# Attention matmuls pinned among the layers' units, and a query side laid out by unit

## The chip, the cores and the metric

The kernel runs on one core of one Trainium2 chip. The metric is the device time of one execution in microseconds (us). Engines: PE is TensorE's matmul, PEld its weight load, DVE is VectorE, ACT is ScalarE, POOL is GpSimd, SP is SyncE, which issues the DMAs.

## The reference

Linear attention over 4 batches of 8 heads, 576 positions, head size 64, followed by two feed-forward layers on the 2304 tokens:

```python
def phi(x):
    proj = x @ w_phi                                   # 64 -> 128
    proj = proj - max(abs(proj), axis=-1)
    return concat([exp(proj), exp(-proj)])             # 256 features
q_p, k_p = phi(q), phi(k)
kv  = k_p^T @ v ;  z = sum_s k_p                       # per batch and head
attn = (q_p @ kv) / (q_p @ z + 1e-6)
x  = attn as (tokens, 512)
x  = leaky_relu(x @ w_in, 0.01) @ w_out                # 512 -> 2048 -> 512
out = (silu(x @ w_gate) * (x @ w_val)) @ w_out2        # 512 -> 1536 -> 512
```

The weights of the two layers arrive as 64-bit floats, everything else as 32-bit floats.

## The kernel before, in words

**Units.** The layers are cut into 272 units, in an order written out by hand (lines 620 to 658): per batch 16 units of the first product (`u_l1`), 12 pairs of gate and value units (`u_gate`, `u_val`), and after every fourth hidden block four units of the output product (`u_out`). Every unit is 24 matmuls of 128x288 in two halves of 12 (`products`, line 543), each half into one of the four PSUM buffers of the tag `pm`; the second half's first matmul opens its second buffer. Operands are kept as a rounded part and a remainder, and three of the four products of parts are made. Batch 0 owns units 0 to 63, batch 1 units 64 to 131, batch 2 132 to 199, batch 3 200 to 267; the last four finish batch 3.

**Weights.** In batch 0 every weight block comes as 64-bit numbers and is turned to 32 bits and split by ACT and DVE (`w_to_f32`, lines 504 to 522: two ACT and three DVE instructions of 128x512; `w_split`, lines 524 to 532: one of each), about one block a unit, up to four units ahead of its use. From batch 1 on the split blocks are read back from DRAM, so this work is gone.

**Attention.** Batch 0 is computed before unit 0. Batches 1 to 3 are computed beside the units of the batch before. The key side (`k_steps`, line 249) has 24 steps: `k_front` makes one block of features (PE, then DVE for the maximum, ACT for the exponentials), `k_back` two steps later sums it into the key-value product, `k_z` and `k_tr` finish a head pair. Batch 1 keeps its operands whole (`whole`, line 103), so each of its feature matmuls shows as two records; batches 2 and 3 split them. The query side of batches 1 to 3 (`q_steps_t`, line 439) goes over 8 groups (4 head pairs by 2 halves of the positions): `q_p` projects (line 334 and 335, two banks) and turns the result on DVE; `q_m_t` forms the maximum: one small matmul (line 344), four DVE instructions (lines 346 to 354) that end in the tile `mrow`; `q_exp` subtracts it by a matmul (line 365) and takes two exponentials on ACT (lines 373 and 374); `q_num` multiplies with the key-value product (line 391); `q_fin` divides.

**PSUM.** The attention of batches 1 to 3 uses four buffers of the tag `pa` (`bk`, line 93). `q_p` holds two of them from its matmul until the exponentials of `q_exp` have read them; each `q_num` holds one until `q_fin` has read it.

**Where the steps stand.** `spread` (line 685) gives each step a unit after which it is written: for batch 1 the key steps behind units 0 to 23 and the query steps behind units 24 to 60; for batches 2 and 3 behind the first 32 units of the batch before and the 33 that follow. `q_steps_t` makes 20 steps, two per group (`q_p` and `q_m_t` of one group, `q_exp` of the group before, `q_num` of the one before that), so a step is 1.85 units in batch 1 and 1.65 in the others.

**What sets the order.** A planner orders each engine's instructions. It takes, of those that its own timeline holds ready, the one with the lowest priority number, which is the place in the program; attention steps are written with the number lowered by 50 (line 718). An issue-order token keeps all instructions that carry it in program order on their engine. Before the change only the first matmul of each half unit carries the token "units":

```python
m = pe.matmul(ps, w, x[:, c], start=(i == 0), stop=(i == n - 1))
if i == 0:
    tc.stamp_issue_order_token(m.ins, "units")
```

So the units stay in order among themselves, and an attention matmul may go ahead of its place or behind it. On the chip every engine then runs its list in order.

Of the kernel before, what the change touches and what calls it, by code (L numbers as in the profile page):

```python
# [19 lines left out]
F = 128  # L20
# [19 lines left out]
def linear_attention_two_mlps(ctx: ExitStack, tc, qT, kT, vt, w_phi, w1, w2, wg, wv, w3, cst, out):  # L40
# [35 lines left out]
    def constants():  # L76
# [13 lines left out]
        dve.tensor_copy(sel, signs)  # L90
        dve.tensor_scalar(out=ones, in0=zero, scalar1=1.0, scalar2=None, op0=ALU.add)

    def bk(b=1):

        if b == 0:
            return T([P, 512], F32, "pm", 4, psm)
        return T([P, 512], F32, "pa", 4, psa)
# [51 lines left out]

    def k_front(b, j, s):  # L150
        ps = bk(b)
        o = slice(OFF[s], OFF[s] + P)
        pv = ps[:, 0 : 2 * F]
        if whole(b):
            ops = [(raw["k", b, j], wbd)]
        else:
            ops = [(kh[b, j], wbd_h), (kl[b, j], wbd_h), (kh[b, j], wbd_l)]
        for i, (a, w) in enumerate(ops):
            pe.matmul(  # L159
                pv, a[:, o], w.rearrange("p h f -> p (h f)"), start=(i == 0), stop=(i == len(ops) - 1)  # L160
            )
        pv = pv.rearrange("p (h f) -> p h f", h=2)
        mk = T([P, 2], F32, "mk", 2)
        dve.tensor_reduce(out=mk, in_=pv, axis=AX.X, op=ALU.max, apply_absolute_value=True)
        f = ff[b, j, s] = T([P, 2, 2, F], F32, "ff", 3)
        if b in (1, 2):
            mn = T([P, 2], F32, "mn", 2)
            dve.tensor_scalar(out=mn, in0=mk, scalar1=-1.0, scalar2=None, op0=ALU.mult)
            for h in range(2):
                act.activation(f[:, h, 0], pv[:, h], AF.Exp, bias=mn[:, h : h + 1])  # L170
                act.activation(f[:, h, 1], pv[:, h], AF.Exp, bias=mk[:, h : h + 1], scale=-1.0)
        else:
            d = f[:, :, 1]
            sub(d, pv, mk.rearrange("p (h o) -> p h o", o=1).to_broadcast([P, 2, F]))
            act.activation(f[:, :, 0], d, AF.Exp)
            act.activation(f[:, :, 1], d, AF.Exp, scale=-1.0)
        if whole(b):
            return
        hh = fh[b, j, s] = T([P, 2, 2, F], F32R, "fh", 3)
        ll = fl[b, j, s] = T([P, 2, 2, F], F32R, "fl", 3)  # L180
        cp(hh, f)
        sub(ll, f, hh.bitcast(F32))
        if s == 1:
            z = zacc[b, j] = T([P, 2, 2, F], F32, "zacc", 1)
            dve.tensor_tensor(out=z, in0=ff[b, j, 0], in1=f, op=ALU.add)
        elif s > 1:
            z = zacc[b, j]
            n = VAL[s]
            dve.tensor_tensor(out=z[:n], in0=z[:n], in1=f[:n], op=ALU.add)

    def k_back(b, j, s):
        if s == 0:
            kvp[b, j] = bk()
        ps = kvp[b, j]
        n = VAL[s]
        v = vaug.pop((b, j, s)) if whole(b) else vhl[b, j][:, s]
        for h in range(2):
            parts = (ff,) if whole(b) else (fh, fl)
            for i, part in enumerate(parts):
                pe.matmul(  # L200
                    ps[:, 256 * h : 256 * h + 256],
                    v[:n, h].rearrange("p a d -> p (a d)"),
                    part[b, j, s][:n, h].rearrange("p a f -> p (a f)"),
                    start=(s == 0 and h == 0 and i == 0),
                    stop=(s == NST - 1 and i == len(parts) - 1),
                    skip_group_check=True,
                )

    def z_split(b, j):
        if whole(b):  # L210
# [8 lines left out]
    def k_z(b, j):  # L219
        ps = kvp.pop((b, j))  # L220
        kz = kvz[b, j] = T([P, 512], F32, "kvz", 1)
        if whole(b):
            cp(kz, ps)
            return
        zh, zl = zhl.pop((b, j))
        tb = T([D, 512], F32, "ff", 3)
        cp(tb, ps[D:P])
        dve.tensor_tensor(out=kz[0:D], in0=ps[0:D], in1=tb, op=ALU.add)
        zp = bk()
        pe.matmul(zp, ones, zh, start=True, stop=False)  # L230
        pe.matmul(zp, ones, zl, start=False, stop=True)
        cp(kz[D:P], zp[D:P])

    def k_tr(b, j):
        kz = kvz.pop((b, j))
        ps = bk()
        for i in range(4):
            pe.transpose(ps[:, F * i : F * i + F], kz[:, F * i : F * i + F], ident)  # L238
        if whole(b):
            kvh[b, j] = T([P, 2, 2, P], F32, "kvh", 4)  # L240
            cp(kvh[b, j].rearrange("p h a f -> p (h a f)"), ps)
            return
        h = kvh[b, j] = T([P, 2, 2, P], F32R, "kvh", 4)
        l = kvl[b, j] = T([P, 2, 2, P], F32R, "kvl", 4)
        pv = ps.rearrange("p (h a f) -> p h a f", h=2, a=2)
        cp(h, pv)
        sub(l, pv, h.bitcast(F32))
# [78 lines left out]
    def q_p(b, j, t):  # L326

        c = slice(HT * t, HT * t + HT)
        tp = T([P, 2, NB, 32], F32, "pk", 5)
        for h in range(2):  # L330
            bank = pt[b, j, h, t] = bk(b)
            ps = bank[:, 0:HT]
            a = qs[b, j][h][:, c]
            pe.matmul(ps, wst_h, a, start=True, stop=False)  # L334
            pe.matmul(ps, wst_l, a, start=False, stop=True)  # L335
            dve.transpose(out=tp[:, h].rearrange("p a b -> p (a b)"), in_=ps)
        m = mq[b, j, t] = T([P, 2, NB], F32, "mqt", 2)
        dve.tensor_reduce(out=m, in_=tp, axis=AX.X, op=ALU.max, apply_absolute_value=True)

    def q_m_t(b, j, t):  # L340

        m = mq.pop((b, j, t)).rearrange("p h k -> p (h k)")
        turned = pt[b, j, 1, t][0 : 2 * NB, HT : HT + P]
        pe.matmul(turned, m, ident, start=False, stop=True, skip_group_check=True)  # L344
        top = T([2 * NB, 32], F32, "top", 2)
        dve.tensor_reduce(out=top, in_=turned.rearrange("r (g i) -> r i g", g=4), axis=AX.X, op=ALU.max)
        x = mm[2 + t]
        hi = x[0 : 2 * NB]
        dve.tensor_copy(hi, top)
        sub(x[32 : 32 + 2 * NB], top, hi.bitcast(F32))  # L350
        if t == 0:
            mrow[b, j] = T([P, 2 * NB, 32], F32R, "mrow", 1)
        r = mrow[b, j][:, NB * t : NB * t + NB]
        dve.tensor_tensor(
            out=r,
            in0=x.bitcast(F32).rearrange("p (o i) -> p o i", o=1).to_broadcast([P, NB, 32]),
            in1=mask_t.rearrange("p (k o) -> p k o", o=1).to_broadcast([P, NB, 32]),
            op=ALU.mult,
        )

    def q_exp(b, j, h, t):
        if lean(b):
            ps = pt.pop((b, j, h, t))[:, 0:HT]
            r = mrow[b, j][:, NB * t : NB * t + NB].rearrange("p k i -> p (k i)")
            pe.matmul(ps, sel[:, 2 + h], r, start=False, stop=True, skip_group_check=True)  # L365
        else:
            ps = bk()[:, 0:HT]
            c = slice(HT * t, HT * t + HT)
# [14 lines left out]
    def q_num(b, j, h, t):  # L383
# [4 lines left out]
        if not whole(b):  # L388
            ops += [(kvl[b, j][:, h, s], hh[:, s]) for s in range(2)]
        for i, (w, x) in enumerate(ops):  # L390
            pe.matmul(ps, w, x, start=(i == 0), stop=(i == len(ops) - 1))  # L391
        if h == 0:
            dn[b, j, t] = T([P, HT], F32, "dn", 2)
        act.activation(dn[b, j, t][D * h : D * h + D], ps[D:P], AF.Copy, bias=1e-6)  # L394
# [20 lines left out]
        sub(xl[b, j][:, c], x, xh[b, j][:, c].bitcast(F32))  # L415

    def q_steps(b):
        if lean(b):
            return q_steps_t(b)
        seq = []  # L420
        for j in range(NP):
            seq.append([lambda j=j: q_front(b, j, 0), lambda j=j: q_front(b, j, 1)])
# [13 lines left out]
            seq.append(prev)  # L436
        return seq

    def q_steps_t(b):


        groups = [(j, t) for j in range(NP) for t in range(2)]
        n = len(groups)
        steps = []
        for i in range(n + 2):
            one, two = [], []
            if i >= 2:
                j, t = groups[i - 2]
                one.append(lambda j=j, t=t: q_num(b, j, 0, t))
                two.append(lambda j=j, t=t: (q_num(b, j, 1, t), q_fin(b, j, t)))  # L450
            if 1 <= i <= n:
                j, t = groups[i - 1]
                one.append(lambda j=j, t=t: q_exp(b, j, 0, t))
                two.append(lambda j=j, t=t: q_exp(b, j, 1, t))
            if i < n:
                j, t = groups[i]
                if t == 0:
                    one.append(lambda j=j: q_split(b, j))
                one.append(lambda j=j, t=t: q_p(b, j, t))
                two.append(lambda j=j, t=t: q_m_t(b, j, t))  # L460
                if t == 1 and j + 1 < NP:
                    two.append(lambda j=j: load_q(b, j + 1))
                if t == 1 and j + 1 == NP and b + 1 < B:
                    two.append(lambda: load_k(b + 1, 0))
            steps += [one, two]
        return steps


    wtile, w64, wf = {}, {}, {}
# [220 lines left out]
    for b in range(B - 1):  # L690
        first, mid, end = bounds[b]
        if b == 0:
            mid -= 4
        spread(k_steps(b + 1), first, mid)
        spread(q_steps(b + 1), mid, end - 3)

    load_k(0, 0)
    steps = k_steps(0) + q_steps(0)
# [95 lines left out]
```

## Time and profile before

| | |
|---|---|
| median of 3 runs | 1112.93 us (1109.64 to 1115.9) |
| profiled execution | 1116.18 us, span 1114.3 us |
| PE, PEld busy | 1084.8 us (97%), 1047.4 us (94%) |
| DVE, ACT busy | 708.7 us (64%), 564.4 us (51%) |
| DMA | 203.60 MB, mean 183 GB/s |
| mean granted TensorE clock | 0.994 |

The shares are means over stages that differ: attention of batch 0 alone up to about 65 us; units 0 to 23 with the key side of batch 1 to 188 us; units 24 to 63 with its query side to 365 us; then batches 1 and 2 of the layers with the attention of batches 2 and 3; and from about 881 us layers alone. Busy time of PE includes the overlap of matmuls that follow each other, so a PE that is busy all the time may still have waited a little. A granted clock of 1.00 is 2.4 GHz, 0.50 is 1.2 GHz.

### The profile page before, as it was taken

The numbers are of one execution on the slowest core, as the hardware profiler recorded it, in microseconds if no ns is written. First come the engines' busy times: TensorE is split into PE (matmuls) and PEld (weight loads), VectorE is DVE, ScalarE is ACT, GpSimd is POOL, SyncE is SP. The second block draws the span as 40 slices with busy tenths as digits, with TensorE's granted clock in tenths as the row PEclk, the third lists the DMA queues.
The fourth block names the chain that finished last, engine by engine and source line by source line (L and its number), as shares of the span: only waits on it lengthen the run. The fifth ranks groups of instructions, "written<-read, shape, count | busy, mean of one in ns | idle before, by whom it ended". The sixth has DMA issues, their size and how long they took to land.

```text
span 1114.3 us, 19823 instructions
## 1 busy us (share of the span) xinstructions
PE 1084.8 (97%) x7728; PEld 1047.4 (94%) x7728; DVE 708.7 (64%) x1505; ACT 564.4 (51%) x1259; POOL 6.6 (1%) x28
## 2 busy tenths in 40 slices
PE   7899999999899999999999999999999999999998
PEld 6778999888898999999999999999999999999998
DVE  7887797998989656566675766637676412233233
ACT  7768886766657566544553466525543222222211
POOL 1000000000000000000000000000000000000000
PEclk9999999999999999999999999999999999999999
DMA  9626787667767843455342555434243454455541
GB/s 337 213 71 223 254 292 256 208 241 255 248 207 249 288 157 128 153 181 181 136 147 92 184 193 175 152 133 164 94 176 121 168 184 152 164 198 169 178 144 43
DMA packets 70476, 203.60 MB, mean 183 GB/s; under 512 B 17264, under 2 KB 17520, under 8 KB 70384
## 3 DMA queue, kind: packets, MB, share of 16 engines
q1 hardware_dynamic: 70384, 202.35, 52.6%
q8 instruction: 61, 1.00, 0.4%
q14 instruction: 31, 0.25, 0.1%
HBM read 159.86 MB, written 42.47 MB: 182 GB/s over the span
## 4 chain that ended last, share of the span: by engine, by line
PE 85%; DMA 5%; DVE 4%; ACT 4%; issue 1%; SPq 0%; ACTq 0%; DVEq 0%
PE pm L550 72%; PE pa L391 4%; PE pa L200 3%; DMA wi<-in_w_dram 2%; PE pa L159 2%; PE pm L299 1%; DVE wr L521 1%; PE pa L334 1%; PE pa L344 1%; PE pa L238 1%; PE pa L365 1%; DMA wi<-in_wv_dram 1%; DVE wr L516 1%; PE pa L335 1%; PE pa L370 0%
## 5 line engine op out<-in xcount | busy, mean ns | idle before, releaser
L550 PE MATMUL pm<-xh,wi 128*128 128x288 f32 x2560 | 539.3, 299 | 3.5 <-DVE es L581 1.1
L550 PEld LDWEIGHTS pm<-xh,wi 128*128 128x128 f32 x2560 | 420.3, 190 | 9.1 <-ACT xh L60 2.6
L550 PE MATMUL pm<-gp,wo 128*128 128x288 f32 x2688 | 389.5, 296 | 1.7 <-ACT wo L529 1.5
L550 PE MATMUL pm<-xl,wi 128*128 128x288 f32 x1280 | 379.8, 298 | 0.2 <-DVE xl L57 0.2
L550 PEld LDWEIGHTS pm<-gp,wo 128*128 128x128 f32 x2688 | 367.4, 188 | 5.1 <-ACT wo L529 1.8
L550 PEld LDWEIGHTS pm<-xl,wi 128*128 128x128 f32 x1280 | 242.5, 190 | 1.8 <-DVE xl L57 0.6
L57 DVE TENSOR_TENSOR gp<-es,gp 128x576 fp32r<-128x576 f32 x112 | 84.4, 753 | 98.4 <-ACT gp L60 98.1
L60 ACT ACTIVATE gp<-es 128x576 fp32r<-128x576 f32 x112 | 77.4, 691 | 92.5 <-DVE es L588 91.1
L607 DVE TENSOR_TENSOR acc<-pm,acc 128x288 f32<-128x288 f32 x160 | 70.6, 453 | 81.9 <-PE pm L550 81.3
L573 ACT ACTIVATE es<-pm 128x288 f32<-128x288 f32 x128 | 53.0, 417 | 104.2 <-PE pm L550 103.5
L588 DVE SCALAR_TENSOR_TENSOR es<-pm,es 128x288 f32<-128x288 f32 x96 | 43.3, 452 | 52.8 <-PE pm L550 52.1
L581 DVE SCALAR_TENSOR_TENSOR es<-es,pm 128x288 f32<-128x288 f32 x96 | 43.2, 450 | 34.1 <-ACT es L580 32.1
L57 DVE TENSOR_TENSOR fl<-ff,fh 128x512 fp32r<-128x512 f32 (+1 forms) x72 | 51.4, 716 | 18.5 <-ACT fh L60 17.5
L580 ACT ACTIVATE es<-pm 128x288 f32<-128x288 f32 x96 | 39.0, 409 | 41.8 <-PE pm L550 40.9
L514 ACT ACTIVATE wi<-wi 128x512 int32<-128x512 uint32 x62 | 43.0, 693 | 31.9 <-DMA wi<-in_w_dram 18.8
L60 ACT ACTIVATE fh<-ff 128x512 fp32r<-128x512 f32 (+1 forms) x72 | 47.5, 663 | 0.9
L394 ACT ACTIVATE dn<-pa 64x288 f32<-64x288 f32 x64 | 26.0, 406 | 42.3 <-PE pa L391 41.3
L513 ACT ACTIVATE wr<-wi 128x512 f32<-128x512 f32 x62 | 41.4, 689 | 11.3 <-DMA wi<-in_w_dram 7.2
L200 PE MATMUL pa<-ff,pk 128*128 128x256 f32 (+1 forms) x160 | 43.0, 384 | 4.0 <-issue 3.0
L521 DVE TENSOR_TENSOR wr<-wr,wi 128x512 uint16<-128x512 uint16 x62 | 46.2, 752 | 0.6
L60 ACT ACTIVATE acc<-pm 128x288 f32<-128x288 f32 x64 | 26.0, 422 | 33.4 <-PE pm L550 33.2
L516 DVE SCALAR_TENSOR_TENSOR wr<-wi,wr 128x512 int32<-128x512 int32 x62 | 42.3, 686 | 0.9
(107 smaller groups left out, 1183.6 us busy)
## 6 DMA issues: line engine op xcount, KB each, us to landing
wi<-kept SPq DMA_DIRECT2D x120, 512.0 KB, 3.5
wo<-kept SPq DMA_DIRECT2D x82, 512.0 KB, 5.4
wi<-in_w_dram SPq DMA_DIRECT2D x46, 512.0 KB, 5.0
kept<-wi SPq DMA_DIRECT2D x40, 512.0 KB, 4.2
kept<-wo SPq DMA_DIRECT2D x28, 512.0 KB, 4.9
wi<-in_wv_dram SPq DMA_DIRECT2D x12, 512.0 KB, 4.3
raw<-in_kT_dram SPq DMA_DIRECT2D x16, 288.0 KB, 3.2
raw<-in_qT_dram SPq DMA_DIRECT2D x16, 288.0 KB, 2.8
```

The costliest lines, as they stand in the source:

```text
L57: dve.tensor_tensor(out=o, in0=a, in1=b, op=ALU.subtract)
L60: act.activation(o, a, AF.Copy)
L200: pe.matmul(ps[:, 256 * h : 256 * h + 256], v[:n, h].rearrange("p a d -> p (a d)"), part[b, j, s][:n, h].rearrange("p a f -> p (a f)"), st ...
L391: pe.matmul(ps, w, x, start=(i == 0), stop=(i == len(ops) - 1))
L514: act.activation(low, low.bitcast(U32), AF.Copy, scale=2.0**-29)
L516: dve.scalar_tensor_tensor(out=ti, in0=high, scalar=-0x80000000, in1=ti, op0=ALU.bitwise_and, op1=ALU.bitwise_or)
L521: dve.tensor_tensor(out=t16, in0=t16, in1=e16, op=ALU.add)
L550: m = pe.matmul(ps, w, x[:, c], start=(i == 0), stop=(i == n - 1))
L573: act.activation(g[:, c], ps, AF.Prelu, alpha=0.01)
L581: dve.scalar_tensor_tensor(out=t[:, c], in0=t[:, c], scalar=1.0, in1=ps, op0=ALU.add, op1=ALU.mult)
L588: dve.scalar_tensor_tensor(out=g[:, c], in0=ps, scalar=0.5, in1=g[:, c], op0=ALU.mult, op1=ALU.mult)
L607: dve.tensor_tensor(out=acc[o][:, t], in0=ps, in1=acc[o][:, t], op=ALU.add)
```

## The change

`pinned` gives the token "units" to every attention matmul of batches 1 to 3: of the key side (`k_front`, `k_back`, `k_z`, `k_tr`) and of the query side (`q_p`, `q_m_t`, `q_exp`, `q_num`). Each then stands, in program order, behind the second half's first matmul of the unit after which it is written and ahead of the next unit's first matmul. The ACT, DVE and DMA instructions carry no new token.

The query side is no longer written as 20 steps. `q_places` gives each operation a place of its own, in periods of (hi - lo) / 8.5 units: 4.35 units in batch 1, 3.88 in batches 2 and 3. In periods from the group's start: `q_p` 0, `q_m_t` 0.27, both `q_exp` 0.75, `q_num` 1.27 and 1.47, `q_fin` 1.48. In batch 1 this puts `q_m_t` one unit behind `q_p`, `q_exp` two units behind `q_m_t` (three once), the first `q_num` two units behind `q_exp` (three once), and the next group's `q_p` one unit (two once) behind `q_exp`. Key steps keep their places.

```diff
+    def pinned(b, m):
+        if b:
+            tc.stamp_issue_order_token(m.ins, "units")
...
-            pe.matmul(
+            m = pe.matmul(
                 pv, a[:, o], w.rearrange("p h f -> p (h f)"), start=(i == 0), stop=(i == len(ops) - 1)
             )
+            pinned(b, m)
...
-            pe.matmul(ps, wst_h, a, start=True, stop=False)
-            pe.matmul(ps, wst_l, a, start=False, stop=True)
+            pinned(b, pe.matmul(ps, wst_h, a, start=True, stop=False))
+            pinned(b, pe.matmul(ps, wst_l, a, start=False, stop=True))
...
-    def q_steps_t(b):
+    def q_places(b, lo, hi):
         groups = [(j, t) for j in range(NP) for t in range(2)]
...
+        period = (hi - lo) / (len(groups) + 0.5)
+        out = []
+        for g, (j, t) in enumerate(groups):
+            if t == 0:
+                out.append((g, lambda j=j: q_split(b, j)))
+            out.append((g, lambda j=j, t=t: q_p(b, j, t)))
+            out.append((g + 0.27, lambda j=j, t=t: q_m_t(b, j, t)))
+            if t == 1 and j + 1 < NP:
+                out.append((g + 0.4, lambda j=j: load_q(b, j + 1)))
+            if t == 1 and j + 1 == NP and b + 1 < B:
+                out.append((g + 0.4, lambda: load_k(b + 1, 0)))
+            for h in range(2):
+                out.append((g + 0.75, lambda j=j, h=h, t=t: q_exp(b, j, h, t)))
+                out.append((g + 1.27 + 0.2 * h, lambda j=j, h=h, t=t: q_num(b, j, h, t)))
+            out.append((g + 1.48, lambda j=j, t=t: q_fin(b, j, t)))
+        out.sort(key=lambda p: p[0])
+        return [(int(lo + at * period), fn) for at, fn in out]
...
         spread(k_steps(b + 1), first, mid)
-        spread(q_steps(b + 1), mid, end - 3)
+        for at, fn in q_places(b + 1, mid, end - 3):
+            atts.setdefault(at, []).append([fn])
```

The matmuls of `k_back`, `k_z`, `k_tr`, `q_m_t`, `q_exp` and `q_num` are wrapped in the same way as those shown. No instruction is added or taken away on any engine.

## Rows read from the trace of the kernel before

**Rows 1.** Stages: stretch; busy us (instructions) of PE, PEld, DVE, ACT, POOL; clock; DMA.
```profile
65.00:125.00 60.00, 56.79 (x324) 48.83 (x324) 47.28 (x110) 47.28 (x129) 1.66 (x6) 1.00 0.54 180
125.00:188.00 63.00, 63.00 (x449) 61.62 (x448) 53.04 (x102) 51.06 (x114) 0.20 (x1) 1.00 0.83 294
...
202.00:365.00 163.00, 150.80 (x1009) 141.87 (x1008) 147.50 (x319) 106.22 (x217) 0.00 (x0) 0.96 0.69 237
365.00:484.00 119.00, 119.00 (x909) 118.65 (x908) 67.92 (x136) 67.56 (x171) 0.00 (x0) 1.00 0.54 189
484.00:622.00 138.00, 138.00 (x1029) 135.03 (x1028) 95.43 (x210) 62.56 (x135) 0.00 (x0) 1.00 0.42 137
...
900.00:1100.00 200.00, 200.00 (x1510) 199.97 (x1509) 58.94 (x111) 49.52 (x100) 0.00 (x0) 1.00 0.46 159
```

**Rows 2.** PE's waits, 202 to 365 us: total us, times, longest us.
```profile
PE pa L334 <- ACT ff L374: 4.4, 3, 3.2
PE pa L365 <- DVE mrow L354: 2.5, 1, 2.5
PE pm L550 <- ACT wo L529: 1.5, 1, 1.5
PE pa L391 <- DVE xf L409: 1.3, 1, 1.3
PE pm L550 <- DVE es L581: 1.1, 1, 1.1
```

**Rows 3.** Stage table again, three short stretches; the clock stands behind POOL.
```profile
243.40:246.70 3.30, 3.16 (x13) 3.16 (x14) 1.81 (x4) 3.27 (x9) 0.00 (x0) 0.50 0.72 288
304.90:311.60 6.70, 5.66 (x23) 5.67 (x24) 4.66 (x10) 6.32 (x13) 0.00 (x0) 0.50 0.52 191
352.70:356.00 3.30, 3.30 (x16) 3.30 (x15) 2.87 (x9) 3.27 (x12) 0.00 (x0) 0.50 1.01 411
```

**Rows 4.** Timeline, a `q_m_t` of batch 1: start us, us, engine, line, [idle before].
```profile
236.04 0.39 PE L344 MATMUL pa<-cst_sb,mqt 128*18 128x128 f32 x2
...
243.04 0.45 DVE L354 TENSOR_TENSOR mrow<-mm,cst_sb 128x288 fp32r<-128x288 f32 x1
...
243.54 0.85 PE L365 MATMUL pa<-mrow,sel 128*128 128x288 f32 x2 [2.50 <-DVE mrow L354]
```

**Rows 5.** Timeline around the longest wait for a bank.
```profile
299.38 0.29 PE L365 MATMUL pa<-mrow,sel 128*128 128x288 f32 x1
...
305.48 0.41 ACT L374 ACTIVATE ff<-pa 128x288 f32<-128x288 f32 x1
...
305.94 0.61 PE L334 MATMUL pa<-pk,wst_h 128*128 128x288 f32 x1 [3.16 <-ACT ff L374]
```

**Rows 6.** Timeline, the latest `mrow` and the latest reduction of batch 1's groups.
```profile
255.30 0.39 PE L344 MATMUL pa<-cst_sb,mqt 128*18 128x128 f32 x2
...
264.90 0.45 DVE L354 TENSOR_TENSOR mrow<-mm,cst_sb 128x288 fp32r<-128x288 f32 x1
...
311.62 0.32 PE L335 MATMUL pa<-pk,wst_l 128*128 128x288 f32 x1
...
315.06 0.71 DVE L338 TENSOR_REDUCE mqt<-pk 128x18 f32<-128x576 f32 x1
```

**Rows 7.** PE's groups by line, 65 to 125 us, key side: count, busy us, mean ns, idle.
```profile
L200 PE MATMUL pa<-ff,pk 128*128 128x256 f32 (+1 forms) x44 | 12.2, 384 | 1.3 <-issue 1.3
...
L159 PE MATMUL pa<-wbd,raw 128*128 128x256 f32 x28 | 8.5, 392 | 0.2 <-DVE xf L409 0.2
```

**Rows 8.** Timeline: one front and the next, a back between them.
```profile
111.33 0.60 PE L159 MATMUL pa<-wbd,raw 128*128 128x256 f32 x2
111.77 1.03 PE L200 MATMUL pa<-ff,pk 96*128 96x256 f32 x4
112.63 0.60 PE L159 MATMUL pa<-wbd,raw 128*128 128x256 f32 x2
```

**Rows 9.** PE's groups by line, 202 to 365 us: fronts of batch 2.
```profile
L159 PE MATMUL pa<-wbd_h,pk 128*128 128x256 f32 x10 | 2.0, 280 | 0.0
```

More of the change, by code (lines that the diff above doesn't have):

```diff
@@ L199, in k_back @@
             for i, part in enumerate(parts):
-                pe.matmul(
+                m = pe.matmul(
                     ps[:, 256 * h : 256 * h + 256],
@@ L207, in k_back @@
                 )
+                pinned(b, m)
     def z_split(b, j):
@@ L229, in k_z @@
         zp = bk()
-        pe.matmul(zp, ones, zh, start=True, stop=False)
-        pe.matmul(zp, ones, zl, start=False, stop=True)
+        pinned(b, pe.matmul(zp, ones, zh, start=True, stop=False))
+        pinned(b, pe.matmul(zp, ones, zl, start=False, stop=True))
         cp(kz[D:P], zp[D:P])
@@ L237, in k_tr @@
         for i in range(4):
-            pe.transpose(ps[:, F * i : F * i + F], kz[:, F * i : F * i + F], ident)
+            m = pe.transpose(ps[:, F * i : F * i + F], kz[:, F * i : F * i + F], ident)
+            pinned(b, m)
         if whole(b):
@@ L343, in q_m_t @@
         turned = pt[b, j, 1, t][0 : 2 * NB, HT : HT + P]
-        pe.matmul(turned, m, ident, start=False, stop=True, skip_group_check=True)
+        pinned(b, pe.matmul(turned, m, ident, start=False, stop=True, skip_group_check=True))
         top = T([2 * NB, 32], F32, "top", 2)
@@ L364, in q_exp @@
             r = mrow[b, j][:, NB * t : NB * t + NB].rearrange("p k i -> p (k i)")
-            pe.matmul(ps, sel[:, 2 + h], r, start=False, stop=True, skip_group_check=True)
+            pinned(b, pe.matmul(ps, sel[:, 2 + h], r, start=False, stop=True, skip_group_check=True))
         else:
@@ L390, in q_num @@
         for i, (w, x) in enumerate(ops):
-            pe.matmul(ps, w, x, start=(i == 0), stop=(i == len(ops) - 1))
+            pinned(b, pe.matmul(ps, w, x, start=(i == 0), stop=(i == len(ops) - 1)))
         if h == 0:
@@ L417, in q_steps @@
     def q_steps(b):
-        if lean(b):
-            return q_steps_t(b)
         seq = []
@@ L437, in q_steps @@
         return seq
-    def q_steps_t(b):
+    def q_places(b, lo, hi):
         groups = [(j, t) for j in range(NP) for t in range(2)]
[L443 to L466, printed above, removed]
+        period = (hi - lo) / (len(groups) + 0.5)
[15 more added lines that the diff above has]
+        return [(int(lo + at * period), fn) for at, fn in out]
     wtile, w64, wf = {}, {}, {}
```

## The prediction

> **What bounds the kernel now.** I read the stage table first, because the page's totals are means over stages that differ. From 365 us on PE is busy without a break, and from 900 to 1100 us it does 1510 matmuls in 200 us, 0.1325 us each, so a unit of 24 takes 3.18 us [rows 1]. Nothing can be gained there by order. The same holds for 125 to 188 us. Two stretches have holes: 65 to 125 us, where PE is idle for 3.2 of 60 us, and 202 to 365 us, the units 28 to 63 with most of batch 1's query side, where it is idle for 163 - 150.8 = 12.2 us [rows 1]. In that long stretch DVE is busy for 147.5 of 163 us: it has the weights of batch 0 to convert beside the attention. In the query stage of batch 2 it is busy for 95.4 of 138 us, and PE never stops [rows 1]. So the holes belong to a stage where DVE is nearly full.
>
> Second, PE's waits in the stretch. Three are those of attention matmuls: `q_p` for a bank that the exponentials still read (4.4 us in three times), `q_exp` for `mrow` (2.5 us, once), `q_num` for a bank (1.3 us), 8.2 us together. The units' own waits are smaller, such as 1.5 us for a weight block and 1.1 us for DVE [rows 2].
>
> Third, the clock. In three short stretches the granted clock is 0.50, and matmuls then take twice as long: 13 records in 3.3 us, 23 in 6.7 us, 16 in 3.3 us [rows 3]. The first begins at the end of the 2.50 us wait for `mrow` [rows 4], the second within the 3.16 us wait for a bank [rows 5]. PE had been idle ahead of both; no stretch without such a hole shows it. At half speed 3.3 + 6.7 + 3.3 = 13.3 us hold the work of about half of that, so the three cost some 6.7 us, the first two 5.0 us.
>
> Here the Trainium skill (Perfetto Trace Analysis, Identifying the Most-Contended Engine) would have me look elsewhere: matmul busy time is a poor measure of what TensorE has left, the busy share of weight loads a better one. The weight loads of the stretch are busy for 141.9 of 163 us against 118.65 of 119 in the next one [rows 1], so by that rule some 21 us are open instead of 12.2. My 12.2 plus 6.7 for the clock makes 18.9, so the trace bears the rule out for this stretch: the difference is the half clock, which busy time hides. By the rule alone the floor would be 1112.9 - 21 = 1092 us.
>
> **The change, part by part.** No instruction comes or goes. What changes is PE's order and, through the planner, the order on ACT and DVE.
>
> *The query side of batch 1.* Before, `q_p` of a group is written right behind the `q_exp` of the group before, and needs a bank which that one's exponentials read: it waits at once when they are late. After, it stands one unit or more behind, and the `q_num` of the older group have by then given back their two banks, at their `q_fin` 0.52 period earlier. The banks that the exponentials read are wanted next by the group's own `q_num`, 0.52 period or 2.26 units or 7.2 us behind `q_exp`. In the longest case the last exponential ended 305.89 - 299.38 = 6.5 us after its matmul [rows 5], so this wait goes. `q_exp` gets two units behind `q_m_t`, 6.4 us, and two `q_num` of four records between; four records of 256 columns take 0.86 us [rows 8], so four of 288 an estimated 0.97, and the room is 8.3 us. Of the eight groups the latest `mrow` is ready 265.35 - 255.69 = 9.7 us after the small matmul [rows 6], the one that PE waited for 243.49 - 236.43 = 7.1 us [rows 4]. I let one group in eight stay late by 9.7 - 8.3 = 1.4 us and add 0.3 us for a second. `q_m_t` gets one unit behind `q_p`, 3.2 us; the latest reduction of the eight ends 315.77 - 311.94 = 3.8 us after `q_p` [rows 6]. The 0.6 us over can be made up, since a pinned matmul may still slide behind the eleven free matmuls of the half unit in which it stands (1.5 us). So the 8.2 us of waits and the 5.0 us of half clock behind them go, 13.2 us, and 1.7 us come back: **-11.5 us**.
>
> What is late next is DVE. It idles for 15.5 us in the stretch [rows 1], so a gain of 11.5 us wants it busy for 147.5 of 151.5 us. The pin helps a little: five fronts of batch 2 (15 matmuls) stand in this stretch, ahead of unit 64 where they are written [rows 9], and go behind 365 us, where DVE has 57% [rows 1]; their DVE work goes with them. The units' waits for weights and DVE [rows 2] stay, and with them the third half clock.
>
> *The key side of batch 1.* Now attention runs ahead of its places: between 65 and 125 us, while units 0 to 7 run, stand 28 records of fronts and 44 of backs, so 14 fronts and 11 backs [rows 7]. By their places only 8 fronts and 6 backs may be there. So 6 fronts and 5 backs move behind 125 us, into a stretch where PE is full [rows 1]. A back of four records takes 112.63 - 111.77 = 0.86 us, a front 0.44 us [rows 8]: 6 x 0.44 + 5 x 0.86 = 6.9 us of PE work. What they cost is what the first stretch doesn't give back. There PE is busy for 56.8 of 60 us, ACT and DVE for 47.3 [rows 1], so it is mostly PE that sets its length, and it should shorten by most of the 6.9 us. The bounds are -3.2 us, if its idle time goes too because the backs then come with more room behind their fronts, and +6.9 us, if it keeps its length. I take **+1.5 us**, nearer to the row of PE than to that of the two others.
>
> *Batches 2 and 3.* PE has no hole today, so the sum here is nothing or a loss. The places give the same room in units, and DVE has 69% and 57% there [rows 1]. Bounds: 0, and 1.7 us for each batch if it behaved as batch 1. I take **+1.0 us** for both.
>
> *The loads.* The DMA issues on SP move with their steps: the next batch's first `load_k` comes five units later in batch 1, still eight units or 25 us ahead of its pinned front, and the weight loads on the same queue don't wait for it. Nothing.
>
> Sum: -11.5 + 1.5 + 1.0 = -9.0 us on the profiled execution, 1116.2 to 1107.2 us. That execution lies 3.25 us above the median of the three runs, 1112.93, so **1104 us**.
>
> **Rivals.**
> *DVE sets the stage's length anyway.* [...] The attention's waits would come back as waits of the units for weights and for banks that DVE empties. Against it: of PE's 12.2 us idle 8.2 are attention's and 4.0 the rest's, and while PE stands DVE is not fed either. If the 8.2 us come back as many short waits, only the 5.0 us of half clock are gained and the 2.5 us of the other parts lost: 1112.9 - 5.0 + 2.5 = 1110 us.
>
> *Slower: ready attention can no longer fill holes.* The place is units 0 to 8. Before, a front or back that is ready goes ahead while a unit waits for its weight block; after, it has to stand behind that unit. Price: all of the 6.9 us, if the stretch keeps its length because ACT and DVE (79% each) set it [rows 1], and likewise the query side's gain fails because a late `mrow` now holds the units behind it. Then 1112.9 + 6.9 + 1.0 = 1121 us. It decides alone once the query side's gain is under 2.3 us; with more than that the kernel stays within 0.5%. Against it: of the 3.2 us idle there 1.5 stand ahead of fronts and backs themselves [rows 7], so the units waited for at most 1.7.
>
> *The units' waits go too.* If smoother attention on ACT and DVE brings weights earlier, all of the 12.2 us and all three half clocks go: 18.9 us, 1094 us.
>
> That the pins do nothing is excluded by the places: fronts of batch 2 stand before the unit behind which they are written [rows 9].
>
> **How the numbers follow.** Forecast 56% (1099 to 1109 us), DVE 24% (1107 to 1114), slower 14% (1116 to 1124), units' waits too 6%. A measurement of this kernel tells a change of about 0.5% (5.6 us) from none: faster is below 1107.4, slower above 1118.5. Faster: 7 of 8 of the forecast (0.49), all of the last (0.06), an eighth of DVE's (0.03): 0.58. Slower: most of the third, 0.13. The rest, 0.29, is no change. The range takes in the last case's upper part and the third's centre, from 1095 to 1121 us; the forecast's own is 1099 to 1109.
>
> **What would show it right or wrong.** Right: in the stretch of units 28 to 63 no wait of line 334 on line 374 and none over 1.5 us of line 365 on `mrow`; at most one short stretch at clock 0.50; the stretch shorter by 9 to 12 us, with DVE at 95% or more; units 0 to 23 longer by 0 to 3 us; from 365 to 881 us no idle time of PE over 0.3 us at one place, and no front of batch 2 ahead of unit 64. Wrong: the stretch stays above 160 us with DVE waiting on ACT and units waiting on weights (first rival), or units 0 to 23 take 5 us more (second).

## The result, and the profile after

The change makes the kernel 0.75% slower: 1122.33 us median (1118.65 to 1125.24, 7 runs) against 1113.58 us (1109.64 to 1115.9, 7 runs), a ratio of 1.0075 (95% interval 1.0052 to 1.0098). The profiled execution took 1123.08 us, its span is 1121.3 us, 7.0 us more than before. A stage reaches from the start of its first unit's first matmul to that of the next stage's:

| units | before, us | after, us | difference |
|---|---|---|---|
| ahead of unit 0 | 65.8 | 66.5 | +0.7 |
| 0 to 7 | 59.3 | 56.5 | -2.8 |
| 8 to 23 | 63.1 | 71.1 | +8.0 |
| 24 to 27 | 14.0 | 14.0 | 0 |
| 28 to 63 | 162.5 | 159.2 | -3.3 |
| 64 to 95 | 119.8 | 121.7 | +1.9 |
| 96 to 131 | 137.5 | 138.7 | +1.2 |
| 132 to 199 | 259.4 | 260.8 | +1.4 |
| 200 to the end | 232.9 | 232.8 | -0.1 |

The stage table of the changed kernel (columns as in [rows 1]; the stages 0 to 7, 8 to 23, 28 to 63 and 64 to 95):

```profile
66.50:123.00 56.50, 49.52 (x285) 44.41 (x284) 46.45 (x100) 42.80 (x107) 0.83 (x3) 0.94 0.59 198
123.00:194.00 71.00, 70.37 (x481) 67.52 (x481) 51.93 (x109) 55.18 (x133) 1.30 (x4) 1.00 0.73 257
208.00:367.00 159.00, 146.52 (x987) 137.86 (x987) 144.63 (x310) 102.56 (x206) 0.00 (x0) 0.97 0.70 240
367.00:489.00 122.00, 122.00 (x934) 121.64 (x932) 71.90 (x144) 72.17 (x182) 0.00 (x0) 1.00 0.54 189
```

In the first row PE idles for 7.0 of 56.5 us and the clock is 0.94, where [rows 1] show 3.2 of 60 us at 1.00. In the third it idles for 12.5 us, against 12.2 before.

PE's groups by line in units 0 to 7 show that the places hold: 16 records of fronts and 24 of backs, which is 8 fronts and 6 backs, for 28 and 44 in [rows 7].

```profile
L550 PE MATMUL pm<-xh,wi 128*128 128x288 f32 x80 | 18.7, 311 | 6.0 <-ACT wi L529 5.7 <-ACT es L573 0.3
...
L206 PE MATMUL pa<-ff,pk 128*128 128x256 f32 (+1 forms) x24 | 7.2, 426 | 0.0
L164 PE MATMUL pa<-wbd,raw 128*128 128x256 f32 x16 | 5.2, 411 | 0.0
```

The timeline has one hole there, of 5.42 us ahead of unit 4's first matmul:

```profile
96.90 0.29 PE L550 MATMUL pm<-xh,wi 128*128 128x288 f32 x1
...
98.49 0.67 ACT L514 ACTIVATE wi<-wi 128x512 int32<-128x512 uint32 x1 [1.30 <-DMA wi<-in_w_dram]
...
101.90 0.66 ACT L529 ACTIVATE wi<-wr 128x512 fp32r<-128x512 f32 x1
...
102.61 0.61 PE L550 MATMUL pm<-xh,wi 128*128 128x288 f32 x1 [5.42 <-ACT wi L529]
```

Unit 4 waits for its weight block, the sixth in the order of the blocks. Its conversion had ended at 89.8 us:

```profile
89.08 0.74 DVE L521 TENSOR_TENSOR wr<-wr,wi 128x512 uint16<-128x512 uint16 x1
```

Its split (line 529) came only at 101.9 us. In ACT's list it stands behind the first instructions on later blocks, the ninth and the tenth if loads and conversions are counted in order, which waited 1.30 us (the line at 98.49) and 0.59 us for their raw forms. The unit starts 2.2 us earlier than before (102.6 for 104.8 us from the start), so the block is not late by itself. Before, PE had used that time for fronts and backs, and only 0.25 us of the wait were left:

```profile
104.78 0.40 PE L550 MATMUL pm<-xh,wi 128*128 128x288 f32 x1 [0.25 <-ACT wi L529]
```

PE's waits in units 28 to 63, against [rows 2]:

```profile
PE pm L550 <- ACT wi L529: 6.5, 4, 2.5
PE pm L550 <- ACT wo L529: 2.5, 2, 1.7
PE pa L352 <- DVE mqt L346: 2.3, 1, 2.3
PE pm L550 <- DVE wi L57: 1.0, 1, 1.0
PE pa L373 <- DVE mrow L362: 0.2, 1, 0.2
```

Attention's waits went from 8.2 to 2.5 us, and what is left is `q_m_t` (line 352 now). The waits of units for weight blocks (`wi`, `wo`) are 10.0 us; before, all that was not attention's came to 4.0, of which 2.6 were for blocks. The blocks themselves come hardly sooner than before. A block is ready when ACT has split it; this is the 63rd of the 70 splits, of the block of unit 61, in the kernel before and in the changed one:

```profile
348.12 0.63 ACT L529 ACTIVATE wi<-wr 128x512 fp32r<-128x512 f32 x1 [0.56 <-DVE wr L521]
```
```profile
354.09 0.62 ACT L529 ACTIVATE wi<-wr 128x512 fp32r<-128x512 f32 x1
```

Unit 28 starts at 202.2 us before and at 208.1 us after, so this split ends 146.5 and 146.6 us behind its start, and in both kernels unit 61 starts 0.1 us after the split. The blocks of units 37, 51 and 63 were split 0.4, 0.1 and 0.3 us ahead of their units before; after, each 0.1 us ahead. Measured from unit 28 in the same way, the 30th to the 68th split (from the start of this stage to just behind its end) come 1.0 us earlier than before on average.

And the stretches at the half clock, against [rows 3]:

```profile
100.80:107.40 6.60, 4.79 (x15) 4.26 (x16) 4.00 (x8) 6.15 (x14) 0.00 (x0) 0.50 0.87 329
216.90:220.00 3.10, 3.10 (x14) 2.92 (x14) 1.94 (x5) 1.44 (x3) 0.00 (x0) 0.50 0.77 225
251.00:254.20 3.20, 3.20 (x11) 2.63 (x10) 3.10 (x6) 2.61 (x5) 0.00 (x0) 0.50 0.85 338
333.00:336.10 3.10, 3.10 (x13) 3.10 (x14) 1.94 (x5) 0.87 (x2) 0.00 (x0) 0.50 0.40 149
```

The first begins within the hole of unit 4. In units 28 to 63 there are 9.4 us of them instead of 13.3.

### The profile page after: what moved, and what is told of

It reads as the page before. It is cut to its first block, busy times and chain, and to the rows that moved or that the text cites. A ratio compares the mean times of both kernels' runs of the same rounds, so it can differ in the third digit from the quotient of the medians.

```text
span 1121.3 us, 19764 instructions
## 1 busy us (share of the span) xinstructions
PE 1085.6 (97%) x7728; PEld 1049.0 (94%) x7728; DVE 708.9 (63%) x1505; ACT 561.0 (50%) x1259; POOL 6.9 (1%) x28
## 4 chain that ended last, share of the span: by engine, by line
PE 84%; DVE 7%; DMA 4%; ACT 3%; issue 1%; SPq 0%; ACTq 0%; DVEq 0%
PE pm L550 70%; PE pa L206 3%; PE pa L399 3%; PE pa L164 2%; DMA wi<-in_w_dram 2%; DMA kept<-wi 1%; DVE wr L516 1%; DVE wr L521 1%; DMA wi<-in_wv_dram 1%; PE pm L307 1%; PE pa L352 1%; DVE wi L57 1%; PE pa L245 1%; ACT wr L513 0%; PE pa L373 0%
## 5 line engine op out<-in xcount | busy, mean ns | idle before, releaser
L550 PE MATMUL pm<-xh,wi 128*128 128x288 f32 x2560 | 524.8, 296 | 14.6 <-ACT wi L529 12.2
L550 PEld LDWEIGHTS pm<-xh,wi 128*128 128x128 f32 x2560 | 414.2, 188 | 21.0 <-ACT wi L529 13.8
L550 PE MATMUL pm<-gp,wo 128*128 128x288 f32 x2688 | 383.8, 298 | 3.1 <-ACT wo L529 2.5
L176 ACT ACTIVATE ff<-pa,mn 128x128 f32<-128x128 f32 x80 | 29.4, 367 | 29.6 <-DVE mn L174 15.0
```

## The experiments

All ratios are to the kernel before, on the same chip, with 95% intervals. The stage lengths come from one profiled execution each. Theory A, with which I began: the key pins keep ready attention out of the holes of units 0 to 8, and DVE, full with the weights, decides the query stage. Theory B blamed the query side, theory C the pins on it. Theory F, formed after e8, says that weight blocks come only just in time because their buffers do. D, E, G and H are rivals that the expectations explain. Where the text says how much earlier the blocks come, it means the 30th to the 68th split, counted from the start of unit 28 and against the kernel before.

**e1, key pins alone.** The kernel before with `pinned` in `k_front`, `k_back`, `k_z` and `k_tr` only.

Its edit against the changed kernel, with the old `q_steps_t` put back and the rest of the query side treated like the line shown:

```diff
+    def unpinned(b, m):
+        return m
...
-            pinned(b, pe.matmul(ps, wst_h, a, start=True, stop=False))
+            unpinned(b, pe.matmul(ps, wst_h, a, start=True, stop=False))
...
-        for at, fn in q_places(b + 1, mid, end - 3):
-            atts.setdefault(at, []).append([fn])
+        spread(q_steps_t(b + 1), mid, end - 3)
```

> The kernel before with the key side's matmuls pinned and the query side left as it was. Theory A (the key pins take ready attention out of holes of units 0 to 8, and the query side only trades one wait for another): units 0 to 24 take about 5 us more than before, as in the changed kernel; unit 28 to 64 some 2 us less, because five fronts of batch 2 go behind unit 64, which costs the same 2 us there; 1118 to 1121 us in all. Theory B (the new query places and pins are what costs): units 0 to 24 as before or 1 us more, 1112 to 1115 us.

Measured: 1121.05 us, ratio 1.0052 (1.0032 to 1.0071). The two stages of units 0 to 23:

```profile
66.20:122.30 56.10, 49.04 (x285) 43.91 (x284) 46.41 (x99) 42.73 (x107) 0.83 (x3) 0.94 0.59 199
122.30:193.80 71.50, 70.76 (x486) 68.23 (x486) 52.80 (x110) 55.30 (x133) 1.04 (x4) 1.00 0.72 258
```

Together 127.6 us, as in the changed kernel, for 122.4 before. This is theory A: the key pins alone bring this loss.

**e2, the query side alone.** The changed kernel without `pinned` in those four functions.

> The changed kernel without the pins of the key side: query side pinned and at its new places. Theory A: units 0 to 24 take what they took before (122 us), the stretch of units 28 to 64 is 159 to 163 us with the units waiting for weight blocks where attention waited before, batches 2 and 3 of the query side lose about 1 us each; 1112 to 1116 us. Theory B: 1119 to 1123 us.

Measured: 1115.64 us, ratio 1.0008 (0.9993 to 1.0022): no change. Units 0 to 23 take 122.2 us, units 28 to 63 159.8 us with 9.1 us of waits for weight blocks:

```profile
PE pm L547 <- ACT wi L526: 6.8, 4, 3.2
PE pm L547 <- ACT wo L526: 1.9, 2, 1.7
PE pm L547 <- DVE wi L57: 0.4, 2, 0.2
```

Theory A again: the query side by itself gains 2.7 us in its stage and gives it back in batches 2 and 3 (1.5 and 1.4 us in units 96 to 131 and 164 to 199).

**e3, places without pins.**

```diff
     def pinned(b, m):
-        if b:
+        if False:
```

> The new query places with no pin at all. Theory A (DVE sets the length of units 28 to 64 whatever the order): that stretch 157 to 163 us, PE idle 8 us or more in it, all in all 1110 to 1115 us. Theory C (the places give the room and the pins take it away by holding the units): the stretch 150 us or less, 1102 to 1106 us.

Measured: 1121.99 us, ratio 1.0065 (1.0047 to 1.0084). Neither theory's number: units 28 to 63 take 170.6 us.

```profile
205.30:375.90 170.60, 154.55 (x1023) 144.74 (x1022) 156.01 (x339) 114.26 (x245) 0.00 (x0) 0.95 0.68 230
```

1023 matmuls stand there for 987 in the changed kernel, and DVE has 156 us to do for 145: without pins still more of batch 2 is drawn into the stage where DVE is full. Theory C falls.

**e4, pins on the old steps.** In the second step of each pair `q_exp` is put ahead of `q_num`, so that four banks suffice.

The first cut is against the changed kernel, the second against the old steps:

```diff
-        for at, fn in q_places(b + 1, mid, end - 3):
-            atts.setdefault(at, []).append([fn])
+        spread(q_steps_t(b + 1), mid, end - 3)
...
-                two.append(lambda j=j, t=t: q_exp(b, j, 1, t))
+                two.insert(0, lambda j=j, t=t: q_exp(b, j, 1, t))
```

> All pins with the query side in its 20 old steps; in each second step the exponentials stand ahead of the product, since four banks don't hold the old order when it is fixed. Theory A: units 0 to 24 as in the changed kernel (5 us over before); in units 28 to 64 waits of the projection for a bank and of the subtraction for its maxima that hold the units, 160 us or more; 1118 to 1126 us. Theory C: the same or worse than the changed kernel by more than 5 us, since the places are what helps: 1127 us or more.

Measured: 1145.16 us, ratio 1.0272 (1.0251 to 1.0293); units 28 to 63 take 172.9 us, and the query stages of batches 2 and 3 142.9 us each for 137.5 and 137.2. PE's longest waits between 200 and 370 us:

```profile
PE pa L342 <- ACT ff L382: 7.5, 6, 2.0
PE pa L399 <- DVE xf L417: 7.3, 2, 5.5
```

The time is theory C's (1127 us or more), far beyond the 1118 to 1126 of theory A, whose waits of the projection for a bank are there all the same. Beside pins the new places are worth 172.9 - 159.2 = 13.7 us in this stage, against old steps with one pair of operations swapped: pins need the places, and places (e3) need the pins.

**e5, key pins with earlier places.** Key steps of batch 1 behind units 0 to 11, two a unit.

```diff
-        spread(k_steps(b + 1), first, mid)
+        spread(k_steps(b + 1), first, first + 12 if b == 0 else mid)
```

> The changed kernel with the key steps of batch 1 written behind units 0 to 11, two a unit, instead of behind 0 to 23; all pins stay. If the loss of units 0 to 24 is pinned work kept out of holes (theory A), the wait of unit 4 for its weight block (5.4 us in the changed kernel) shrinks to 2 us or less, the first eight units carry again about 27 us of attention on PE, and units 0 to 24 take 121 to 124 us; 1114 to 1118 us in all. If the pin itself costs, because a late back holds the units wherever it stands (theory E), PE waits for exponentials in lines 206 or 245 for 3 us or more in units 0 to 12 and units 0 to 24 stay at 127 us or more; 1121 us or more.

Measured: 1116.02 us, ratio 1.0035 (1.0022 to 1.0048) for the changed kernel's 1.0075, some 4.5 us less. The same two stages, now 121.6 us:

```profile
66.20:127.00 60.80, 58.66 (x341) 51.55 (x339) 49.91 (x117) 52.92 (x142) 1.87 (x7) 1.00 0.58 201
127.00:187.80 60.80, 60.04 (x426) 57.64 (x425) 46.17 (x89) 43.66 (x98) 0.00 (x0) 1.00 0.76 268
```

PE is idle for 2.1 us in the first one, and unit 4 waits no more. In these units a pin as such costs nothing; what cost is that ready matmuls were kept out of the hole.

**e6, the query change for batch 1 alone.** e2 with old steps and no pins for batches 2 and 3.

> Query pins and new places for batch 1 alone; key side free, batches 2 and 3 as in the kernel before. Adding stage lengths of the runs so far: units 0 to 28 as before, 28 to 64 159.8 us instead of 162.5, batches 2 and 3 as before: 1110 to 1113 us, 0.1 to 0.4% below before. If the loss of the query side of batches 2 and 3 was not from their own pins and places, 1114 to 1117 us.

Measured: 1113.31 us, ratio 1.0003 (0.9988 to 1.0017). Theory A's stages promised a gain of 0.1 to 0.4%; the interval leaves 0.12% at most, so the gain is too small to be told, or none.

**e7 and e8, DVE relieved**, in the kernel before and in the changed one.

```diff
-        dve.tensor_tensor(out=t16, in0=t16, in1=e16, op=ALU.add)
+        dve.tensor_tensor(out=t16[:, 0:64], in0=t16[:, 0:64], in1=e16[:, 0:64], op=ALU.add)
```

> The kernel before, with the 16-bit addition of the weight conversion done on 64 of 512 columns (the low bits of the other columns are left out): about 0.6 us of DVE less for each of 62 blocks, its place in the chain kept. Theory A (DVE, full with the conversion, sets the length of units 28 to 64): the stretch falls from 162.5 to 150 to 156 us, and attention's waits get shorter with it. Theory D (ACT's list, held behind the landing of weight blocks, sets it): 158 us or more.

> The changed kernel with the same thin addition. Theory A: the units' waits for weight blocks in units 28 to 64 fall from some 10 us to 3 us or less, the stretch to 145 to 151 us, and it is shorter than in the thin kernel before, since the new places now can give their room. Theory D: the units still wait for blocks behind ACT for 6 us or more, 155 us or more.

Measured: e7 1104.79 us, ratio 0.9936 (0.9914 to 0.9958); e8 1109.71 us, 0.9973 (0.9956 to 0.9990). Units 28 to 63, e7 first, then e8:

```profile
202.90:351.30 148.40, 143.95 (x1005) 135.57 (x1004) 132.83 (x318) 104.85 (x220) 0.00 (x0) 1.00 0.74 260
```
```profile
200.70:351.00 150.30, 141.92 (x986) 134.83 (x986) 130.57 (x309) 102.00 (x207) 0.00 (x0) 0.99 0.75 260
```

With DVE busy for 133 us instead of 147 the old order loses most of its waits, and none of the stage runs at the half clock. The stage takes 14 us less in e7, more than theory A promised (150 to 156 us). In the changed kernel theory A fails in part. The stage falls by 9 us, but it is not shorter than in e7, and the units still wait for 8.1 us for weight blocks:

```profile
PE pm L550 <- ACT wi L529: 7.3, 4, 2.8
PE pm L550 <- ACT wo L529: 0.8, 1, 0.8
```

DVE's fullness made attention late. It delays the blocks too: in e8 they come 6.5 us earlier than in the kernel before (5.9 us in e7). But the units of the changed kernel are then ready for them earlier as well, and those of units 37, 51 and 63 are again split 0.1 us ahead of their units.

**e9 to e12, six weight buffers.** A raw block, its split form and the blocks in use share five buffers of the tag `wi`. Here there are six, paid for by one of the five intermediate tiles `es`: e9 on the kernel before, e10 on the changed one, e11 on e6, e12 on e8.

```diff
-        wtile[key] = t = T([P, 2, 512], F32R, *(("wo", 5) if key[0] in "23" else ("wi", 5)))
+        wtile[key] = t = T([P, 2, 512], F32R, *(("wo", 5) if key[0] in "23" else ("wi", 6)))
...
-    def w_load(key, tag="wi", n=5):
+    def w_load(key, tag="wi", n=6):
...
-        g = T([P, S], F32, "es", 5)      # and the three other tiles of this tag
+        g = T([P, S], F32, "es", 4)
```

> The kernel before with six instead of five buffers for the gate, value and first-layer weight blocks, raw and split (paid for with four instead of five for the layers' intermediate tile). Theory F (blocks come just in time, because a raw block's load needs a buffer that a unit gives back): the waits in units 28 to 64 are attention's here, so little changes, 158 to 163 us, 1110 to 1114 us. Theory A (only the fullness of DVE counts): the same. A loss of more than 4 us would mean that the fifth intermediate tile mattered.

> The changed kernel with the same six and four buffers. Theory F: the units' waits for weight blocks behind ACT in units 28 to 64 (about 9 us) fall to 4 us or less and the stretch from 159 to 150 to 154 us, the wait of unit 4 (5.4 us) halves; 1110 to 1115 us. Theory A: blocks are late since DVE and ACT convert them late, whatever the buffers; waits 8 us or more, the stretch 157 us or more, 1119 to 1123 us.

> Query pins and places for batch 1 alone, key side free, with six and four buffers: the combination that should beat both kernels if theory F holds. Theory F: units 28 to 64 in 149 to 153 us, 1102 to 1107 us. Theory A: 1110 to 1114 us.

> The changed kernel with six and four buffers and the thin 16-bit addition (64 of 512 columns, the low bits of the others left out). Theory F: with a buffer more and DVE relieved PE is all but free of waits in units 28 to 64, 140 to 144 us (its work there is 138), and 1095 to 1101 us. Theory A: the same as the thin changed kernel with five buffers, 148 to 152 us, 1106 to 1111 us.

Measured: e9 1109.88 us, 0.9967 (0.9951 to 0.9983), with units 28 to 63 in 152.2 us, where theories F and A both said that little changes. e10 1105.63 us, 0.9931 (0.9914 to 0.9948), 145.4 us, its wait for weight blocks 1.4 us and that of unit 4 gone. e11 1105.97 us, 0.9931 (0.9913 to 0.9950). e12 1108.05 us, 0.9943 (0.9923 to 0.9962), 150.4 us where 140 to 144 were expected: a miss. A wait of 2.5 us for a block stands there and 6.8 us at the half clock. The blocks come 12.1 us earlier in e10 and 10.9 in e12, so the relieved DVE brings them no sooner beside a sixth buffer; why isn't settled.

**e13 to e16, which of the two made it.** e13 has four `es` tiles and five weight buffers. e14 to e16 have six weight buffers and five `es`, paid for by one of the two small divisor tiles (`"dn", 2` becomes `"dn", 1`): on the changed kernel, on the kernel before, on e6.

> The changed kernel with four instead of five intermediate tiles and the five weight buffers as they were. Theory F (the sixth weight buffer made the gain of the six-and-four pair): the units' waits for weight blocks in units 28 to 64 stay at 7 us or more, the stretch at 156 us or more; 1119 to 1128 us. Rival G (the gain came from the new plan that any change of buffers brings, or from fewer intermediate tiles): 150 us or less in the stretch, 1105 to 1112 us.

> The changed kernel with six weight buffers, paid for by one instead of two of the query side's small divisor tile; five intermediate tiles. Theory F: units 28 to 64 in 144 to 150 us as with the six-and-four pair, waits for weight blocks 3 us or less; unit 0 starts 4 us earlier than there, so 1100 to 1106 us. Rival G: the stretch 155 us or more, 1114 us or more.

> The kernel before with the same six weight buffers and one divisor tile. Theory F: attention's waits for DVE and ACT in units 28 to 64 are in part left, 150 to 158 us; 1105 to 1110 us, above the changed kernel with the same buffers by 2 to 6 us. Rival G: no order between the two.

> Query pins and places for batch 1 alone, key side free, six weight buffers, one divisor tile. By stage lengths: units 0 to 28 as in the kernel before or some 3 us less, 28 to 64 145 to 151 us, batches 2 and 3 as before: 1099 to 1104 us, the fastest of the set. Rival G: 1108 us or more.

Measured: e13 1122.26 us, 1.0066 (1.0051 to 1.0081), the stretch 160.0 us: nothing of the gain. e14 **1103.65 us, 0.9906 (0.9891 to 0.9922)**. e15 1110.57 us, 0.9964 (0.9949 to 0.9978). e16 1104.31 us, 0.9915 (0.9897 to 0.9933). It is the buffer, as theory F has it, whatever it does: e10 and e14 pay for it with different tiles and share the gain, and e13 pays without it and has none. Shown are units 28 to 63 of e13, the stages of e14 (units 0 to 7, 8 to 23, 28 to 63), then e15's units 28 to 63, then e14's waits between 190 and 370 us, then its 63rd split:

```profile
207.60:367.60 160.00, 147.19 (x990) 138.38 (x989) 145.43 (x312) 102.16 (x207) 0.00 (x0) 0.97 0.69 240
```
```profile
68.60:117.80 49.20, 46.93 (x284) 42.40 (x283) 43.68 (x96) 40.59 (x104) 0.91 (x3) 1.00 0.58 207
117.80:187.70 69.90, 69.90 (x482) 67.63 (x481) 58.02 (x120) 57.95 (x139) 1.03 (x4) 1.00 0.85 298
201.70:348.20 146.50, 141.59 (x987) 134.78 (x986) 137.76 (x299) 97.39 (x198) 0.00 (x0) 0.99 0.69 245
```
```profile
202.20:357.60 155.40, 144.77 (x999) 137.12 (x998) 142.79 (x312) 102.18 (x214) 0.00 (x0) 0.98 0.70 244
```
```profile
PE pa L352 <- DVE mqt L346: 3.2, 3, 1.9
PE pm L550 <- ACT wi L529: 1.5, 1, 1.5
PE pm L550 <- DVE es L581: 0.2, 1, 0.2
```
```profile
333.29 0.63 ACT L529 ACTIVATE wi<-wr 128x512 fp32r<-128x512 f32 x1 [1.06 <-DVE wr L521]
```

Unit 28 of e14 starts at 201.7 us, so this split ends 132.2 us behind it, for 146.6 in the changed kernel; on average the blocks come 12.0 us earlier. Those of units 37, 61 and 63 are now split 5.0, 4.7 and 2.4 us ahead of their units, that of unit 51 still 0.1 us, and for it the unit waits 1.5 us. With a block more in flight the change that cost 0.75% gains: e14 is 6.9 us below e15, which has the same buffers and the old order, and below both kernels. e16 doesn't beat e14, so what the other pins still cost is too small to be told. Units 0 to 23 take 119.1 us in e14 and 119.6 us in e15: the key pins' loss is gone as well, so it was the block's lateness, too. What stays are 1.2 and 1.4 us in the query stages of batches 2 and 3.

One part of e15's expectation failed. The sixth buffer brings the blocks 10.7 us earlier in the old order as well, but there it clears attention's waits, 8.2 us before and 0.5 here, and the units' waits for blocks grow from 2.6 to 7.2 us:

```profile
PE pm L550 <- ACT wi L529: 4.8, 2, 3.9
PE pm L550 <- ACT wo L529: 2.4, 1, 2.4
```

So the buffer loosens the stage as a whole. DVE's work in units 28 to 63, 147.5 us in [rows 1], is 142.8 us in e15 and 137.8 in e14, where part of the conversion has moved to the units ahead. How much of e14's gain comes from that isn't told apart; e8, with 14 us less for DVE and five buffers, gained less and kept its waits for blocks. Nor is it shown how the buffer acts. In units 28 to 63 the loads don't land late: a raw block lies there for 12.7 us on average between its landing and the end of its conversion in the changed kernel, and for 14.3 in e14. At unit 4 the trace points to ACT's list, as theory D has it: in e14 the eighth raw block had landed at 36.1 us, for 93.5 in the changed kernel, and the split of unit 4's block follows its conversion by 3.3 us instead of 12.1.

**e17, more room for the maximum.** e14 with `q_m_t` at 0.50, `q_exp` at 1.00, `q_num` at 1.50 and 1.70, `q_fin` at 1.71.

> The kernel of e14 with q_m_t at 0.50 instead of 0.27 of a period behind q_p, so two units instead of one in most groups, and everything behind it moved by 0.23 to 0.25. Theory H (what is left of attention's waits in units 28 to 64 is the maximum coming one unit behind the projection, 3.2 us in three times in e14): these waits fall below 1 us, the stretch to 142 to 144 us, batches 2 and 3 lose their 0.6 us stall or keep it; 1099 to 1102 us. If DVE is late by the same amount wherever the step stands, the wait stays at 2 us or more or turns up at q_exp; 1103 to 1107 us.

Measured: 1105.09 us, 0.9925 (0.9900 to 0.9950), no better than e14. The wait of line 352 is gone, as theory H had it, but the stretch takes 150.2 us: waits for weight blocks are 3.8 us again, and 6.8 us run at the half clock. One wait went and another took its time; why the blocks come 2.1 us later than in e14 isn't known.

## Why the prediction was wrong

It said 1104 us, and 0.13 for slower. The step that failed is the sentence "The units' waits for weights and DVE [rows 2] stay, and with them the third half clock", on which the -11.5 us of the query side stood; the units' waits went from 4.0 to 10.0 us. A second term was mis-sized, the +1.5 us of the key side, which measured +5.2. In the profiles the sum said -9.0 us and +7.0 came. Of the 16.0 us between, 10.1 are the query side's (-3.3 and +1.9 behind it for -11.5), 3.7 the key side's (+5.2 for +1.5), 1.6 those of batches 2 and 3 and 0.6 the rest.

- *Attention's waits go.* Right: 8.2 to 2.5 us. The 1.7 us that were to come back were priced for `mrow`, which cost 0.2; the room of one unit for `q_m_t`, priced at no wait, was too small by 2.3 us once.
- *The units' waits stay.* Wrong: 4.0 us became 10.0. The weight block that a unit wants was already only just in time. As long as PE stopped for attention, the block came meanwhile; when PE no longer stopped, it reached the unit that much earlier and waited there, since the blocks came only 1.0 us sooner than before. Of the 5.0 us of half clock that were to go some 2 went (13.3 us at 0.50 became 9.4). The stage shortened by 3.3 us, 1.9 of it by fronts and backs of batch 2 that now run behind unit 64 and lengthen units 64 to 95 by as much. This is the first rival's mechanism, attention's waits that come back as the units'. It named DVE alone. The runs show two things that bring the blocks earlier: DVE relieved by 6.5 us (e8), one buffer more by 12.0 us (e14), and only in e14 do the waits for them go.
- *The key side.* The work moved was right: 8 fronts and 6 backs stay, and units 8 to 23 grow by 8.0 us where 6.9 us of work were said to arrive. What the first stage gives back was mis-sized: the sum took +1.5 us of a range from -3.2 to +6.9, because PE was busy for 95% of that stretch, and it was +5.2 (-2.8 and +8.0). PE was busy because attention filled its holes; taken away, the wait for unit 4's block appeared in full, 5.42 us, with 6.6 us at the half clock that begin in it. e1 and e5 show it from both sides. The argument that units had waited for at most 1.7 us there counted what was left of their waits after the filling. Busy time of an engine says what it did, not that it had nothing to wait for.
- *Batches 2 and 3.* +1.0 us predicted; their query stages lost 1.2 and 1.5 us, 0.58 us of each in one wait of a unit for DVE.
- *The loads.* Priced at nothing because weight loads don't wait for the key loads on SP. SP did stand ahead of key loads, 7.4 us in units 28 to 63, but no longer than before (8.4 us), so nothing shows that the price was wrong.
- *The rivals.* The slower one, with 14%, gave 1121 us, and the range ended on it, 1.3 us short. Its first half is what happened: holes that ready attention may not fill. That its sum came so near is in part luck: the query side failed through the blocks and not through a late `mrow` (0.2 us), and units 0 to 23 lost 5.2 us and not 6.9. Of the signs named beforehand its own came true (units 0 to 23 5 us longer); the first rival's bound of 160 us for the stage was missed by 0.8 us.

The rule that the prediction took from the Trainium skill (Perfetto Trace Analysis, Identifying the Most-Contended Engine) agrees with the outcome: weight loads are busy for 87% of the stretch before and after (141.87 of 163 us, 137.86 of 159 us), where little was gained, and for 92% in e14 (134.78 of 146.5 us). Matmul time orders the three alike (93%, 92% and 97%), so these runs don't show which of the two measures is better. The prediction's reading that the difference between them was the half clock is wrong: in [rows 3] weight loads are busy for 12.1 of 13.3 us, just as matmuls are, and e7, with the clock at 1.00 in the stage, has 8.4 us between the two (143.95 and 135.57) for 8.9 in the kernel before.

## What to carry to other kernels

Before a wait is priced as gained, ask for every other input of the same engine how much earlier it could be used: here the weight blocks had no slack beyond the stall that was to go, and of what was tried only a buffer more (three numbers changed) made the new order pay. An order that is fixed keeps ready work out of holes, so place the fixed work where the holes are, as e5 did; and measure a new layout together with the supply that it will want next, not alone.

## What the runs showed of the hardware that was not expected

The half clock follows some holes and not others of the same length. In units 28 to 63 of the changed kernel, holes of 1.7, 2.5 and 2.3 us were each followed by 3.1 to 3.2 us at 0.50, a fourth of 2.0 us was not; in the profile of e6 holes of 2.1, 1.7 and 2.0 us passed with the clock at 1.00 in the whole stage, and that execution's span, 1108.6 us, is that of its shortest run. PE's waits of e6 in that stage:

```profile
PE pm L577 <- ACT wi L556: 6.5, 6, 2.1
PE pa L349 <- DVE mqt L343: 2.0, 1, 2.0
PE pm L577 <- ACT wo L556: 1.7, 1, 1.7
```

One hole of that length isn't needed either: the third stretch of [rows 3], from 352.7 us in the kernel before, follows three small ones, so the prediction's "no stretch without such a hole shows it" doesn't hold for it.

```profile
348.80 0.40 PE L550 MATMUL pm<-xh,wi 128*128 128x288 f32 x1 [0.40 <-ACT wi L529]
350.74 0.37 PE L550 MATMUL pm<-xh,wi 128*128 128x288 f32 x1 [1.14 <-DVE es L581]
351.91 0.53 PE L550 MATMUL pm<-xh,wi 128*128 128x288 f32 x2 [0.67 <-DVE wi L57]
```

So a hole of about 2 us costs itself and, in some executions, some 1.6 us more (half of 3.1 to 3.2 us); what decides it these runs don't show. The scatter of one kernel's runs goes with the clock: of the 87 runs of the kernel before that were made beside the experiments, the five with a mean granted clock of 1.000 took 1109.6 to 1110.7 us, the nine with 0.992 took 1113.8 to 1118.7 us. So stage lengths from one profile say less than the medians do.
